# Chunked attention and a Gelu MLP on one core: k loaded in long runs, transposed by DMA and put in key order by GpSimd

## The chip, the cores and the metric

The kernel runs on one core of one Trainium2 chip. The metric is the device time of one launch in microseconds. The kernel's engines are TensorE (PE in the profile; PEld is its weight load), VectorE (DVE), ScalarE (ACT), GpSimd (POOL) and SyncE (SP), which issues nearly all DMAs; SPq is SP's queue of issues.

## The reference

q, k and v are float32 of shape 8 (batch) x 8 (heads) x 576 (positions) x 64. Attention runs inside chunks of 64 positions, so nine chunks per batch element and head:

```python
scores = (1.0 / np.sqrt(D)) * np.matmul(q_c, k_c.transpose(0, 1, 2, 4, 3))   # per chunk of 64
attn = softmax(scores)                                                        # over the 64 keys
out = np.matmul(attn, v_c)
x = out.transpose(0, 2, 1, 3).reshape(B * S, H * D)                           # 4608 x 512
h = x @ w_in                                                                  # 512 -> 2048
y = gelu_exact(h) @ w_out                                                     # 2048 -> 512
```

## The kernel before

**Tiles.** The 4608 token rows are cut into nine tiles of 512. Tiles 0 to 7 are the first eight chunks of one batch element; tile 8 gathers the ninth chunk of all eight batch elements. For each tile the attention gives x in bfloat16 (`x`, features on partitions); the first product (mm1, `mm1_slot`, L446) gives 16 slices of h, each followed by a Gelu on ScalarE (L448); the second product multiplies h by w_out.

**Order of the work.** The order is written out by hand under a manual schedule: each engine executes its instructions in the order in which the code emits them, and a helper puts the waits in. The main loop over t (L820) runs mm1 of tile t and then its second product in `phase`. The attention of the next tiles is put between the matmuls by two dictionaries: `e1` maps a slice number of mm1 to pieces of work that come ahead of it, `e2` does the same for the steps of the second product. `T0 = 2` is the last tile of a first regime. Tiles 1 and 2 take the attention of tile t+1 in their second product; tile 2 takes the scores of tile 4 at its end as well (step 12), so from tile 3 on the scores (`quad_S`) are two tiles ahead of mm1.

**Second product.** From tile 1 on `mm2_seven` computes the product of 2 x 2 blocks with seven block products instead of eight (steps s = 0 to 6, two sub-steps each, L564). Sums of blocks of h are made by DVE (`g_sum`, L487 and L500; they use s3_sb and the k_bd buffers as room), sums of blocks of w_out once by `weight_sum` (L475, into v_bd, during mm1 of tile 1). `keep` copies a bank of PSUM to an SBUF tile `kept` on ACT (L526), `done` adds a bank to a kept tile on DVE (L531) and stores it (L576). `last` copies the last bank to y_sb on ACT (L536) and stores it; for tile 2 it is put into the list `deferred` and executed ahead of slice 1 of tile 3. The SBUF tiles `kept` and `y_sb` share four buffers.

**The loads of q and k.** `load_qk` brings the float32 data of a tile into a staging buffer (`arrival`, six buffers for all kinds of loads). For q, the position (p j) goes to partition p with j = 4 neighbours in a row: runs of 4 x 64 floats, 1 KB, in one DMA of 1 MB (L114). For k from tile 2 on, `rows_128` (L124) puts the keys on partitions in blocks of 128: four DMAs of 256 KB in runs of 64 floats, 256 bytes; for tile 8 eight DMAs. GpSimd casts both to bfloat16, four instructions per tile and kind (`pool_cast_qk`; L164 for q, L162 for k). `flip` (L194) issues a DMA transpose from SP that puts head dimension on partitions, q_t and k_t with two buffers each. In q_t the positions of a chunk lie as (j, p); in k_t, because of the 128-key blocks, the 64 keys of a chunk lie side by side, and the scores take them as weights directly:

```python
st["kt"][rs, g * J + n, CH * c:CH * (c + 1)]     # L226: 64 keys of a chunk
```

v is loaded in 256-byte runs (`load_v_rows`, nine DMAs per tile) and cast by GpSimd (`cast_v_rows`, L200). Tiles 0 and 1 go another way (`att_Tq`, `att_Tk`: transposes on TensorE).

**Attention of a tile from 2 on.** `quad_S` (L225): 64 matmuls of 64 x 64 into four PSUM banks, exponentials on ACT (L232), partial row sums (`quad_part`, L248 and L251) and totals (`quad_total`) on DVE, or, for tiles 2 and 3, sums by a matmul (`quad_sums`); then `quad_av` (L310) and the product with the reciprocal sums into x (`quad_x`, L317; `quad_x_plain`, L303).

Of the kernel before, what the change touches and what calls it, by code (L numbers as in the profile page):

```python
# [11 lines left out]
def kernel(  # L12
# [10 lines left out]
    P = 128  # L23
# [54 lines left out]

    w_in_sb = consts.tile([P, KS, d_ff], bf16, name="w_in_sb")
    w_out_sb = consts.tile([P, FF, d_model], bf16, name="w_out_sb")  # L80
    w_in_v = moe_w_in.rearrange("(ks p) n -> p ks n", p=P)
    w_out_v = moe_w_out.rearrange("(f p) n -> p f n", p=P)

# [19 lines left out]
    def load_qk(t, nm, h0=0, h1=H):  # L103

        st = tiles[t]
        src = q if nm == "q" else k
        if nm + "f" not in st:
            st[nm + "f"] = stage_tile()[:].rearrange("p (h j d) -> p h j d", h=H, j=J)
            st[nm] = ld.tile([P, G, J, 2, D], bf16, tag=nm, name=f"{nm}_nat")
        raw = st[nm + "f"]  # L110
        if t > 1 and nm == "k":
            rows_128(t, src, raw, False)
        elif t < B:
            nc.sync.dma_start(raw[:, h0:h1], src[t, h0:h1, 0:MT, :].rearrange("h (p j) d -> p h j d", j=J))  # L114
        else:
            for b in range(B):
                nc.sync.dma_start(
                    raw[PC * b:PC * (b + 1), h0:h1],
                    src[b, h0:h1, MT:S, :].rearrange("h (p j) d -> p h j d", j=J))

    def rows_128(t, src, raw, swapped, parity=range(2)):

        def go(to, rows):
            nc.sync.dma_start(to, rows.rearrange("h key d -> key h d"))  # L124
        last = CT // 2 - 1
        if t < B and not swapped:
            for n in range(CT // 2):
                go(raw[:, :, n], src[t, :, P * n:P * (n + 1), :])
        elif t < B and 0 in parity:
            for n in range(CT // 2):  # L130
                go(raw[:, 0::2, n], src[t, 0::2, P * n:P * (n + 1), :])
        if t < B and swapped and 1 in parity:
            for n in range(last):
                go(raw[:, 1::2, n], src[t, 1::2, CH + P * n:CH + P * (n + 1), :])
            go(raw[0:CH, 1::2, last], src[t, 1::2, MT - CH:MT, :])
            go(raw[CH:P, 1::2, last], src[t, 1::2, 0:CH, :])
        if t == B:
            for b in range(B):
                for r in range(2 if swapped else 1):
                    c, n = place(r, b) if swapped else (b % 2, b // 2)  # L140
                    sel = slice(r, H, 2) if swapped else slice(0, H)
                    go(raw[CH * c:CH * (c + 1), sel, n], src[b, sel, MT:S, :])

    def place(r, i):

# [2 lines left out]
    def load_v_rows(t, parity=range(2)):  # L148
        if "vf" not in tiles[t]:
            tiles[t]["vf"] = stage_tile()[:].rearrange("p (h n d) -> p h n d", h=H, d=D)  # L150
        rows_128(t, v, tiles[t]["vf"], True, parity)

    def load_v(t):

# [3 lines left out]

    def cast_qk(t, nm, g, copy):
        st = tiles[t]  # L160
        if t > 1 and nm == "k":
            copy(st[nm][:, :, g], st[nm + "f"][:, :, g].rearrange("p (q r) d -> p q r d", r=2))  # L162
            return
        copy(st[nm][:, g].rearrange("p j r d -> p r j d"), st[nm + "f"][:, 2 * g:2 * g + 2])  # L164

    def cast_v(t, g, r, copies):
# [10 lines left out]

    def att_Tq(t, g, copy):
        tp = transposed(t, "q", g)
        qT = work.tile([P, CT, CH], bf16, tag="qT", name="qT", bufs=5)  # L180
        copy(qT[:].rearrange("p i (c j) -> p i c j", j=J), tp)
        tiles[t]["qT", g] = qT

    def att_Tk(t, g, copy):
# [5 lines left out]

    def flip(t, nm):
        st = tiles[t]
        st[nm + "t"] = flips.tile([P, G * J, P], bf16, tag=nm + "t", name=f"{nm}_t")
        nc.sync.dma_start_transpose(st[nm + "t"][:], st[nm][:].rearrange("p g j r d -> p (g j r d)"))  # L194

    def cast_v_rows(t, copy):
        st = tiles[t]
# [21 lines left out]
    def quad_S(t, banks, later=False, parts=True):  # L219

        st = tiles[t]
        s_ps = four_banks("s_ps", banks)
        for g2, u, g, n, r, c, o, rs, os in quadrants():
            i = 2 * n + c
            nc.tensor.matmul(s_ps[g2][c][os, u, :].rearrange("p (j c) -> p j c", j=J),  # L225
                             st["kt"][rs, g * J + n, CH * c:CH * (c + 1)],  # L226
                             st["qt"][rs, g * J:(g + 1) * J, i * PC:(i + 1) * PC],
                             start=True, stop=True, tile_position=(CH * r, CH * o))
        def exps(g2):
            for c in (1, 0):  # L230
                pT = work.tile([P, CT, CH], bf16, tag="pT", name="pT", bufs=5)
                nc.scalar.activation(pT[:].rearrange("p u (c j) -> p u c j", j=J),  # L232
                                     s_ps[g2][c][:].rearrange("p u (j c) -> p u c j", j=J), Act.Exp, scale=scale)
                st["pT", 2 * g2 + c] = pT
                if parts:
                    quad_part(t, g2, c)
        if later:
            return exps
        for g2 in range(2):
            exps(g2)  # L240
# [213 lines left out]
    HD = d_model // 2  # L454
    HM = MT // P // 2
    ADD, SUB = mybir.AluOpType.add, mybir.AluOpType.subtract
    s3_sb = consts.tile([P, HF, HD], bf16, name="s3_sb")

    def flat(tile, f):
        return tile[:].rearrange("p a b -> p (a b)").rearrange("p (f n) -> p f n", f=f)  # L460
# [38 lines left out]
        b = st["S", 2][part] if b is None else b[:, f]  # L499
        nc.vector.tensor_tensor(st["S", i][part], a, b, op=op)  # L500

    deferred = []

    def mm2_seven(t, hooks):

        st = tiles[t]
# [26 lines left out]

        def last():
            y_sb = ypool.tile([P, HM, HD], f32, tag="y", name="y_sb")
            nc.scalar.copy(y_sb[:], bank["a"][:])  # L536
            store_block(t, 1, 0, y_sb)

        first_done = lambda: done(0, 0, "b", "p1")
        if t <= T0:  # L540
# [5 lines left out]
                 ("d", summed(1), t_sum(1), lambda: keep("p5", "d")),  # L546
                 ("a", summed(3), t_sum(3), lambda: done(1, 1, "a", "p5")),
                 ("d", summed(4), w_block(1, 1), lambda: done(0, 1, "d", "u2")),
                 ("a", raw(1, 1), t_sum(4), (lambda: deferred.append(last)) if t == T0 else last)]
        for s, (name, left, right, then) in enumerate(steps):  # L550
            fresh = name not in bank
            for m in range(HM):
# [143 lines left out]
    with tc.manual_schedule():  # L696
# [114 lines left out]
        def flip_qk(t):  # L811
            for nm in "qk":
                flip(t, nm)

        def bring_qk(t):
            for nm in "qk":
# [3 lines left out]
        for t in range(1, NT):  # L820
# [3 lines left out]
            if t == 1:  # L824
                flip(2, "q")
                load_v_rows(2, (0,))
                flip(2, "k")
                for ms, y_sb in held:
                    store(0, ms, y_sb)
                held.clear()  # L830
                load_v_rows(2, (1,))
            elif t == T0:
                flip_qk(t + 1)
                load_qk(t + 2, "k")
                load_v_rows(t + 1)
                pool_cast_qk(t + 2)
            if n < NT:
                cast_v_rows(n, PO)
            if t == 1:
# [14 lines left out]
            if t <= T0:  # L854
                ov = [lambda m=m: quad_over(n, m) for m in range(G)]
                rx = [[lambda m=m: att_rc(n, m), lambda m=m: quad_x_plain(n, m)] for m in range(G)]
                e2 = {0: [exp, lambda: quad_S(n, ALONE, parts=False)] + g[1][:2], 2: g[1][2:],
                      4: [lambda: quad_sums(n)], 5: [ov[0]], 6: [ov[1]],
                      7: [ov[2], lambda: quad_av(n, ALONE)] + rx[0], 8: [ov[3]] + rx[1], 9: rx[2] + rx[3]}
                if t == 1:  # L860
                    for i, f in ((1, 6), (2, 7), (3, 8), (4, 9)):
                        e1[f] = [lambda i=i: weight_sum(i)] + e1.get(f, [])
                    e2[4].append(lambda: load_qk(4, "q"))
                    e2[11] = [gelu]
                else:
                    e2[12] = [lambda: quad_S(n + 1, ALONE), flip_next, gelu]
            else:
                e2 = {0: g[1][:2], 2: g[1][2:]}
                if n < NT:
                    if t == T0 + 1:  # L870
                        e1[1] = [lambda: deferred.pop()()]
                        e1[3] = [lambda: quad_total(n, DV)]
                    e1[5] = [lambda m=m: quad_rc(n, m // 2, m % 2) for m in range(1, G)]
                    later = []
                    e2 = {0: [exp, lambda: quad_av(n, EVEN if n + 1 < NT else ALONE), xs[0], g[1][0], xs[1], g[1][1]], 2: [flip_next],
                          4: [g[1][2]] + xs[2:],
                          13: [gelu]}
                    if n + 1 < NT:
                        e2[0].append(lambda: later.append(quad_S(n + 1, BESIDE, later=True)))
                        e2[0].append(lambda: later[0](0))  # L880
                        e2[2].append(lambda: later[0](1))
                        e2[10] = [lambda: quad_total(n + 1)]
# [33 lines left out]
```

## Time and profile before

| | |
|---|---|
| median of 3 runs | 279.09 us (278.34 to 282.12) |
| the profiled execution's own time | 278.27 us |
| span of the profiled execution | 276.4 us |
| TensorE busy, granted clock | 264.3 us, 96%; 1.00 |
| DVE, ACT, GpSimd busy | 166.6, 180.1, 92.5 us |
| DMA | 53.92 MB in 123407 packets, 97776 of them under 512 bytes |

The span runs from the first to the last instruction of the profiled execution. The page shows the busy time of each engine, then its busy share in 40 slices of 6.9 us, one digit per slice in tenths; PEclk is the granted TensorE clock. In a timeline a row is: start in us, length in us, engine, line, operation, output<-inputs, count; a bracket gives the idle time of the engine ahead of the row and what ended it. A busy TensorE is not TensorE at its peak, since the ends of matmuls are modelled.

### The profile page before, as it was taken

Reading aid. Unit: us, or ns where it says so; the run is one execution under the profiler, and the core shown is the slowest. Engines: PE = TensorE matmul, PEld = TensorE weight load, DVE = VectorE, ACT = ScalarE, POOL = GpSimd, SP = SyncE. Lnnn points to the kernel's source line nnn. Section 1 sums busy time; section 2 is a strip of 40 time slices with the busy share of each in tenths; the row PEclk is TensorE's granted clock in tenths of the full one; section 3 lists DMA queues with packets and bytes.
Section 4 is the critical chain, followed back from the end, with each engine's and each line's share of the span. In section 5 each row is a group of like instructions: output and inputs, shape, how many; then the busy total and the mean of one; then the engine's idle time right before and its main releaser. Section 6 shows DMA issues by size and latency. Waiting matters only on the chain.

```text
span 276.4 us, 6619 instructions
## 1 busy us (share of the span) xinstructions
PE 264.3 (96%) x2672; PEld 169.2 (61%) x2693; DVE 166.6 (60%) x279; ACT 180.1 (65%) x368; POOL 92.5 (33%) x146
## 2 busy tenths in 40 slices
PE   7699999999989999999989999999999999999994
PEld 2454455447844686458735874588458845874683
DVE  6866348875821679989705991598159915521522
ACT  3866758877846876774577567756776777346610
POOL 7869768832630515306303610451012000000000
PEclk9999999999999999999999999999999999999999
DMA  6999999998899899999999988979430310130014
GB/s 218 273 347 402 392 387 264 235 280 243 209 282 238 193 232 267 247 230 244 183 279 276 205 232 162 185 161 262 117 87 2 116 38 0 40 110 6 0 40 115
DMA packets 123407, 53.92 MB, mean 195 GB/s; under 512 B 97776, under 2 KB 120304, under 8 KB 123376
## 3 DMA queue, kind: packets, MB, share of 16 engines
q1 hardware_dynamic: 123072, 53.23, 75.6%
q8 instruction: 21, 0.34, 0.5%
q10 hardware_dynamic: 304, 0.26, 0.3%
q14 instruction: 10, 0.08, 0.1%
HBM read 36.70 MB, written 9.44 MB: 167 GB/s over the span
## 4 chain that ended last, share of the span: by engine, by line
PE 65%; SPq 15%; DMA 12%; issue 2%; ACT 2%; POOL 2%; DVE 1%; POOLq 0%; ACTq 0%
PE h_ps L446 30%; PE y_ps L564 25%; SPq L124 9%; PE y_ps L634 3%; DMA arrival<-in_q_dram 3%; PE h_ps L436 2%; SPq L157 2%; SPq L114 2%; DMA arrival<-in_moe_w_in_dram 2%; DMA arrival<-in_k_dram 2%; DMA k_t<-k_nat 2%; DMA arrival<-in_v_dram 2%; SPq L194 2%; DMA out_dram<-y_sb 2%; PE y_ps L598 1%
## 5 line engine op out<-in xcount | busy, mean ns | idle before, releaser
L446 PE MATMUL h_ps<-x,w_in_sb 128*128 128x512 bf16 x532 | 118.6, 379 | 1.9 <-ACT h L448 1.0
L448 ACT ACTIVATE h<-h_ps 128x512 bf16<-128x512 f32 x137 | 80.9, 598 | 31.5 <-PE h_ps L446 31.2
L446 PEld LDWEIGHTS <-w_in_sb 128*128 128x128 bf16 x548 | 53.6, 98 | 64.4 <-issue 1.3
L564 PEld LDWEIGHTS <-h 128*128 128x128 bf16 x384 | 36.9, 98 | 6.5 <-issue 1.7
L164 POOL CAST q_nat<-arrival 128x512 bf16<-128x512 f32 x31 | 18.7, 644 | 57.8 <-DMA arrival<-in_q_dram 40.9
L487 DVE TENSOR_TENSOR s_sb<-h 128x2048 bf16<-128x2048 bf16 x8 | 9.7, 1218 | 43.1 <-ACT h L448 43.1
L200 POOL CAST v_nat<-arrival 128x1024 bf16<-128x1024 f32 x14 | 16.8, 1203 | 39.9 <-DMA arrival<-in_v_dram 39.9
L564 PE MATMUL y_ps<-w_out_sb,h 128*128 128x256 bf16 x256 | 29.5, 273 | 0.3 <-issue 0.3
L564 PE MATMUL y_ps<-v_bd,k_bd 128*128 128x256 bf16 x256 | 29.6, 273 | 0.1
L526 ACT COPY kept<-y_ps 128x512 f32<-128x512 f32 (+1 forms) x26 | 14.4, 554 | 23.0 <-PE y_ps L564 22.6
L564 PEld LDWEIGHTS <-k_bd 128*128 128x128 bf16 x256 | 24.8, 98 | 3.4 <-issue 0.5
L162 POOL CAST k_nat<-arrival 128x512 bf16<-128x512 f32 x28 | 21.4, 787 | 9.5 <-DMA arrival<-in_k_dram 9.4
L531 DVE TENSOR_TENSOR kept<-y_ps,kept 128x512 f32<-128x512 f32 (+1 forms) x25 | 16.1, 651 | 12.9 <-PE y_ps L564 7.2
L694 ACT ACT_TABLE_LOAD x18 | 23.1, 1283 | 1.0 <-PEq L900 0.7
L500 DVE TENSOR_TENSOR k_bd<-h 128x1024 bf16<-128x1024 bf16 x16 | 11.5, 721 | 18.5 <-ACT h L448 18.5
L317 DVE TENSOR_TENSOR x<-av_ps,rc 128x512 bf16<-128x512 f32 x20 | 13.3, 685 | 5.2 <-PE av_ps L310 5.2
L232 ACT ACTIVATE pT<-s_ps 128x512 bf16<-128x512 f32 x28 | 14.8, 595 | 2.4 <-PE s_ps L225 2.4
L564 PE MATMUL y_ps<-v_bd,h 128*128 128x256 bf16 x128 | 15.3, 273 | 1.0 <-DVE kept L531 1.0
L564 PE MATMUL y_ps<-w_out_sb,s 128*128 128x256 bf16 x128 | 15.3, 273 | 0.0
L564 PE MATMUL y_ps<-v_bd,s_sb 128*128 128x256 bf16 x128 | 15.3, 273 | 0.0
L251 DVE TENSOR_REDUCE part<-pt 128x16 f32<-128x512 bf16 x20 | 13.7, 686 | 0.7
L564 PEld LDWEIGHTS <-s_sb 128*128 128x128 bf16 x128 | 12.5, 98 | 1.5
(103 smaller groups left out, 294.7 us busy)
## 6 DMA issues: line engine op xcount, KB each, us to landing
arrival<-in_v_dram SPq DMA_DIRECT2D x58, 128.0 KB, 3.1
arrival<-in_k_dram SPq DMA_DIRECT2D x28, 256.0 KB, 6.0
arrival<-in_q_dram SPq DMA_DIRECT2D x7, 1024.0 KB, 6.8
out_dram<-kept SPq DMA_DIRECT2D x21, 256.0 KB, 2.7
arrival<-in_moe_w_out_dram SPq DMA_DIRECT2D x4, 1024.0 KB, 11.6
arrival<-in_moe_w_in_dram SPq DMA_DIRECT2D x6, 512.0 KB, 7.5
out_dram<-y_sb SPq DMA_DIRECT2D x11, 256.0 KB, 2.7
arrival<-in_v_dram SPq DMA_DIRECT2D x28, 64.0 KB, 2.6
```

The source lines that it names most:

```text
L124: nc.sync.dma_start(to, rows.rearrange("h key d -> key h d"))
L162: copy(st[nm][:, :, g], st[nm + "f"][:, :, g].rearrange("p (q r) d -> p q r d", r=2))
L164: copy(st[nm][:, g].rearrange("p j r d -> p r j d"), st[nm + "f"][:, 2 * g:2 * g + 2])
L200: copy(st["v"][:, r::2], st["vf"][:, r::2])
L232: nc.scalar.activation(pT[:].rearrange("p u (c j) -> p u c j", j=J), s_ps[g2][c][:].rearrange("p u (j c) -> p u c j", j=J), Act.Exp, scale ...
L251: nc.vector.tensor_reduce(st["part", g2][:, c, :, :, 0], pt[:].rearrange("p n e u -> p n u e"), axis=mybir.AxisListType.X, op=mybir.AluOpT ...
L446: nc.tensor.matmul(h_ps[:], w_in_sb[:, ks, f * P:(f + 1) * P], tiles[t]["x"][:, ks, :], start=(ks == 0), stop=(ks == KS - 1))
L448: nc.scalar.activation(tiles[t]["h"][:, f, :], h_ps[:], Act.Gelu)
L526: nc.scalar.copy(kept[name][:, ms], ps[:])
L531: nc.vector.tensor_tensor(y_sb[:, ms], ps[:], y_sb[:, ms], op=ADD)
L564: nc.tensor.matmul(to, left(f, m), right[:, f], start=(fresh and (split or m == 0) and f == 0), stop=(f == HF - 1), skip_group_check=True)
L694: nc.scalar.activation(act_scratch[:], rest[:, 0:1], func)
```

## The change

- k of every tile is loaded as q is: one DMA of 1 MB in 1-KB runs (tile 8: eight DMAs), and cast with the instruction form of q.
- After the DMA transpose of k, four GpSimd copies per tile (`k_by_chunk`) write a new tile `k_c` (two buffers) in which the 64 keys of each chunk lie side by side in key order; they read k_t in steps of 128 bfloat16 elements. The scores read k_c. k_t has one buffer instead of two. The copies stand on GpSimd right behind the issue of the transpose in program order, for tile 2 ahead of the casts of v.
- The loads of q and k of tile 4 are both issued at step 4 of tile 1's second product (before: q there, k at the head of tile 2). The casts of tile 4 and the transposes of tile 3 stand at step 10 of tile 1's second product (before: at the head of tile 2). At the head of tile 2 come v's loads and casts of tile 3, then the transposes of tile 4.
- In tile 1 the last of four x products with its broadcast moves from step 9 to step 10.
- `last` of tile 2 is no longer deferred; it is done at once, by DVE. The partial row sums of tile 4 move from right behind its exponentials to ahead of slice 0 of tile 3.
- q transposed of tiles 0 and 1 is kept in s3_sb and not in buffers of its own.

```diff
+    s3_sb = consts.tile([P, FF // 2, d_model // 2], bf16, name="s3_sb")
...
-        if t > 1 and nm == "k":
-            rows_128(t, src, raw, False)
-        elif t < B:
+        if t < B:
             nc.sync.dma_start(raw[:, h0:h1], src[t, h0:h1, 0:MT, :].rearrange("h (p j) d -> p h j d", j=J))
...
-        if t > 1 and nm == "k":
-            copy(st[nm][:, :, g], st[nm + "f"][:, :, g].rearrange("p (q r) d -> p q r d", r=2))
-            return
         copy(st[nm][:, g].rearrange("p j r d -> p r j d"), st[nm + "f"][:, 2 * g:2 * g + 2])
...
-        qT = work.tile([P, CT, CH], bf16, tag="qT", name="qT", bufs=5)
+        qT = s3_sb[:, 2 * g:2 * g + 2].rearrange("p f (i c) -> p (f i) c", c=CH)
...
-        st[nm + "t"] = flips.tile([P, G * J, P], bf16, tag=nm + "t", name=f"{nm}_t")
+        st[nm + "t"] = flips.tile([P, G * J, P], bf16, tag=nm + "t", name=f"{nm}_t", bufs=2 if nm == "q" else 1)
...
+    def k_by_chunk(t, copy):
+        st = tiles[t]
+        st["kc"] = flips.tile([P, G, CT, CH], bf16, tag="kc", name="k_c")
+        for g in range(G):
+            copy(st["kc"][:, g].rearrange("p i (c j) -> p i c j", j=J),
+                 st["kt"][:, g * J:(g + 1) * J].rearrange("p j (i c) -> p i c j", i=CT))
...
-                             st["kt"][rs, g * J + n, CH * c:CH * (c + 1)],
+                             st["kc"][rs, g, i, :],
...
-            nc.scalar.copy(y_sb[:], bank["a"][:])
+            (DV if t == T0 else AC)(y_sb[:], bank["a"][:])
             store_block(t, 1, 0, y_sb)
...
-                 ("a", raw(1, 1), t_sum(4), (lambda: deferred.append(last)) if t == T0 else last)]
+                 ("a", raw(1, 1), t_sum(4), last)]
...
         def flip_qk(t):
             for nm in "qk":
                 flip(t, nm)
+            k_by_chunk(t, PO)
...
                 flip(2, "k")
+                k_by_chunk(2, PO)
...
             elif t == T0:
-                flip_qk(t + 1)
-                load_qk(t + 2, "k")
                 load_v_rows(t + 1)
-                pool_cast_qk(t + 2)
...
-                      7: [ov[2], lambda: quad_av(n, ALONE)] + rx[0], 8: [ov[3]] + rx[1], 9: rx[2] + rx[3]}
+                      7: [ov[2], lambda: quad_av(n, ALONE)] + rx[0], 8: [ov[3]] + rx[1], 9: rx[2], 10: rx[3]}
...
-                    e2[4].append(lambda: load_qk(4, "q"))
+                    e2[4].append(lambda: [load_qk(4, nm) for nm in "qk"])
+                    e2[10] += [lambda: pool_cast_qk(4), lambda: flip_qk(3)]
                     e2[11] = [gelu]
                 else:
-                    e2[12] = [lambda: quad_S(n + 1, ALONE), flip_next, gelu]
+                    e2[9] += e2.pop(10)
+                    e2[12] = [lambda: quad_S(n + 1, ALONE, parts=False), flip_next, gelu]
...
-                        e1[1] = [lambda: deferred.pop()()]
+                        e1[0] = [lambda m=m: quad_part(n, m // 2, m % 2) for m in (1, 0, 3, 2)]
                         e1[3] = [lambda: quad_total(n, DV)]
```

More of the change, by code (lines that the diff above doesn't have):

```diff
@@ L119, in load_qk, with rows_128 @@
                     src[b, h0:h1, MT:S, :].rearrange("h (p j) d -> p h j d", j=J))
-    def rows_128(t, src, raw, swapped, parity=range(2)):
+    def rows_128(t, raw, parity):
         def go(to, rows):
@@ L125, in rows_128 @@
         last = CT // 2 - 1
-        if t < B and not swapped:
+        if t < B and 0 in parity:
             for n in range(CT // 2):
[L128 to L132, printed above, removed]
+                go(raw[:, 0::2, n], v[t, 0::2, P * n:P * (n + 1), :])
+        if t < B and 1 in parity:
             for n in range(last):
-                go(raw[:, 1::2, n], src[t, 1::2, CH + P * n:CH + P * (n + 1), :])
-            go(raw[0:CH, 1::2, last], src[t, 1::2, MT - CH:MT, :])
-            go(raw[CH:P, 1::2, last], src[t, 1::2, 0:CH, :])
+                go(raw[:, 1::2, n], v[t, 1::2, CH + P * n:CH + P * (n + 1), :])
+            go(raw[0:CH, 1::2, last], v[t, 1::2, MT - CH:MT, :])
+            go(raw[CH:P, 1::2, last], v[t, 1::2, 0:CH, :])
         if t == B:
             for b in range(B):
[L139 to L142, printed above, removed]
+                for r in range(2):
+                    c, n = place(r, b)
+                    go(raw[CH * c:CH * (c + 1), r::2, n], v[b, r::2, MT:S, :])
     def place(r, i):
@@ L150, in load_v_rows @@
             tiles[t]["vf"] = stage_tile()[:].rearrange("p (h n d) -> p h n d", h=H, d=D)
-        rows_128(t, v, tiles[t]["vf"], True, parity)
+        rows_128(t, tiles[t]["vf"], parity)
     def load_v(t):
@@ L179, in att_Tq @@
         tp = transposed(t, "q", g)
-        qT = work.tile([P, CT, CH], bf16, tag="qT", name="qT", bufs=5)
-        copy(qT[:].rearrange("p i (c j) -> p i c j", j=J), tp)
+        qT = s3_sb[:, 2 * g:2 * g + 2].rearrange("p f (i c) -> p (f i) c", c=CH)
+        copy(qT.rearrange("p i (c j) -> p i c j", j=J), tp)
         tiles[t]["qT", g] = qT
@@ L456 @@
     ADD, SUB = mybir.AluOpType.add, mybir.AluOpType.subtract
-    s3_sb = consts.tile([P, HF, HD], bf16, name="s3_sb")
     def flat(tile, f):
@@ L500, in g_sum @@
         nc.vector.tensor_tensor(st["S", i][part], a, b, op=op)
-    deferred = []
     def mm2_seven(t, hooks):
```

## The prediction

> **What bounds the kernel now.** First the page: busy time, and TensorE (PE) with its granted clock over the slices.
>
> ```profile
> span 276.4 us, 6619 instructions
> PE 264.3 (96%) x2672; PEld 169.2 (61%) x2693; DVE 166.6 (60%) x279; ACT 180.1 (65%) x368; POOL 92.5 (33%) x146
> PE   7699999999989999999989999999999999999994
> PEclk9999999999999999999999999999999999999999
> ```
>
> PE is never below eight tenths after the start, at full clock. A change that leaves its matmuls alone can only fill or open holes between them. So the second view is the timeline of PE; the bracket is the idle time before a row.
>
> ```profile
> 63.61 0.71 PE L225 MATMUL s_ps<-q_t,k_t 64*64 64x64 bf16 x64
> 77.09 1.91 PE L564 MATMUL y_ps<-v_bd,h 128*128 128x256 bf16 x16 [0.87 <-DVE kept L531]
> 106.22 1.91 PE L564 MATMUL y_ps<-v_bd,h 128*128 128x256 bf16 x16 [0.16 <-DVE kept L531]
> 122.86 0.71 PE L225 MATMUL s_ps<-q_t,k_t 64*64 64x64 bf16 x64 [0.28 <-DMA k_t<-k_nat]
> 139.52 11.38 PE L446 MATMUL h_ps<-x,w_in_sb 128*128 128x512 bf16 x51 [1.03 <-ACT h L448]
> ```
>
> From 19 us on these are the holes, 2.34 us in all: the most that the middle of the kernel can give back, 0.8%. Row one has none: the scores of tile 2 start at 63.61 right behind a matmul. How early was their k? Third view, the timelines of SP, POOL and DVE ahead of 63.61.
>
> ```profile
> 43.51 0.44 SPq L114 DMA_DIRECT2D arrival<-in_q_dram  x1
> 44.06 6.91 SPq L124 DMA_DIRECT2D arrival<-in_k_dram  x4
> 56.07 1.83 SPq L194 DMA_TRANSPOSE k_t<-k_nat  x1
> ...
> 49.25 2.28 POOL L164 CAST q_nat<-arrival 128x512 bf16<-128x512 f32 x4 [0.87 <-DMA arrival<-in_q_dram]
> 51.48 1.23 POOL L162 CAST k_nat<-arrival 128x512 bf16<-128x512 f32 x2
> 52.88 3.16 POOL L162 CAST k_nat<-arrival 128x512 bf16<-128x512 f32 x2 [0.18 <-DMA arrival<-in_k_dram]
> ...
> 52.81 1.21 DVE L475 TENSOR_TENSOR v_bd<-w_out_sb 128x2048 bf16<-128x2048 bf16 x1
> 60.90 0.69 DVE L500 TENSOR_TENSOR k_bd<-h 128x1024 bf16<-128x1024 bf16 x1 [1.51 <-ACT h L448]
> ```
>
> Two casts of k take 0.61 us each; the two beside the weight sums L475 take 1.6 each: GpSimd and a DVE operation with two inputs in SBUF take turns. The transpose is issued at 56.07 and, by the tile view of k_t in this stretch, lands 4.0 later, at 60.1. That is 3.5 us ahead of its use: the slack this change spends.
>
> **The change part by part.** The profiled execution took 278.27 us, span 276.4; the median of the three runs is 279.09, 0.82 above it. I sum changes of the span and put them on the median.
>
> *Loads.* k of tiles 2 to 8 is one 1-MB DMA in 1-KB runs (eight for tile 8), not four in 256-byte runs. SP's issue falls from 6.91 us to about the 0.44 of q. Off PE's path: no PE hole names a load. Worth nothing by itself. The casts keep their number, 4 of 0.61 us per tile: nothing.
>
> *k in key order.* New: 4 GpSimd copies per tile, 128x512 bf16, read in steps of 256 bytes, between the landing of k's transpose and the scores, which now wait for the copies. No row shows such a read on GpSimd. The lower bound is the plain cast of as many elements, 0.61; the upper the longest cast of that shape, 1.61. A read by single elements resembles neither, so I take the middle, 1.11, and keep both. (The Trainium skill, GPSIMD Engine Reference, section 7, says that a GpSimd read with an inner step above 8 bytes costs about 2.9 cycles per element instead of 1.9; at the 1.2 GHz of that page 512 elements are an estimated 1.24 us, and four such copies would make the forecast below 280.3 instead of 279.8. No run so far shows it.) From tile 3 on, cover is there: k of tile 3 lands about 84, its copies follow the casts of tile 4 and end near 90, scores at 92.7; those of tile 5 land near 115, copies end near 119.5, the v casts behind them (2 of 1.04) near 121.6, just ahead of their use at 121.87. Without that cover each late us is a PE us.
>
> *Tile 2, where cover is thin.* (a) k lands whole behind q (49.2): 1.05 MB at the 312 GB/s of the stretch 47 to 50 is 3.4 us, 52.6; at the page's best slice, 402 GB/s, 51.8. Take 52.2, where the first two quarters were there at 51.48. (b) So one cast or two instead of two or more run free of L475 (52.81 on) and the others at 1.6: end between 51.9 + 1.2 + 3.2 = 56.3 and 52.3 + 0.6 + 4.8 = 57.7; take 57.0 (before: 56.04). (c) Transpose 4.0, lands 61.0. (d) Copies: three L500 sums at 60.9 to 63.0 take turns with them; casts beside L500 near 91 us took 1.11 and 1.01 instead of 0.61, so 0.45 more for three of the four: 4 x 1.11 + 1.35 = 5.8, end 66.9. (e) PE reaches the last sixteen score matmuls at 64.05: wait 2.85 us. PE works in order, so everything behind is as much later. Bounds: 56.3 + 4.0 + 4 x 0.61 = 62.7, no wait; 57.7 + 4.1 + 4 x 1.61 + 1.35 = 69.6, wait 5.5. Behind the copies on GpSimd stand v's casts of tile 2 (end near 69; used at 71.0 plus the wait): covered.
>
> *The hole at 77.09.* The last x product (0.69) and its broadcast (0.70) move from step 9 to step 10 of tile 1's second product, behind the sum that frees the bank. DVE reaches that sum at 75 instead of 76.36: -0.87. The x is then written by 77.0, its reader starts at 78: covered.
>
> *The hole at 122.86.* With loads of tiles 4 and 5 issued before the stores, SP is through with the loads of tile 5 and v of tile 4 by about 99 instead of 113; k's transpose of tile 5 waits for the third kept store and goes near 110, not 117.74, and the copies end before 122: -0.28. New there: k_t has one buffer, so SP stands at tile 4's transpose until tile 3's copies are done (near 90), with the loads of tile 5 behind it; they are due after 100.
>
> *The hole at 139.52.*
>
> ```profile
> 133.98 0.55 SPq L576 DMA_DIRECT2D out_dram<-y_sb  x1
> 138.39 0.58 ACT L536 COPY y_sb<-y_ps 128x512 f32<-128x512 f32 x1 [1.49 <-DMA out_dram<-y_sb]
> ```
>
> The deferred block of tile 2 was stored only at 133.98, and ACT waited for its buffer ahead of the Gelus. Now DVE evicts it at once (0.68) and SP stores it before the loads of tile 6. ACT is then free at 136.90; copy 0.58 and Gelu 0.60 end at 138.1, PE needs the bank at 138.5. Against it: DVE's four transposes with sums start behind the eviction (108.8 instead of 106.68), 2.1 us later; idle DVE time of 1.08 at 122.4 and 0.78 at 132.5 takes up most, 0.3 is left, which is the slack. -1.0, bounds 0 and -1.03. qT moves into a buffer that nobody uses until 58 us: nothing.
>
> Sum: -0.87 - 0.28 - 1.0 + 2.85 = +0.7. Median 279.8.
>
> **The rivals.** *In time*: the copies cost what a cast costs and k lands early, PE never waits: 279.09 - 2.15 = 276.9. For it: 3.5 us of slack, 2.43 of plain copies. Against: L475 and L500 stand on both ends. *Slow steps*: the 256-byte step costs several times a plain element. Decides from 2.35 us per copy, where the wait at the scores of tile 2 is 7.8 us (61.0 + 9.4 + 1.35 - 64.05) and the total 5.6 above before, 2%. At 3.0 us the copies end at 74.4, wait 10.3: 287.3. For it: no row of such a read; against: ACT's and DVE's copies of the same permutation (L188, L181: 578, 682 ns) are as quick as plain ones. *The clock falls in the wait*: PE does next to nothing between 63.6 and 66.9, and if it came back at half rate, the 32 matmuls behind it (3.67 us) would take as much again: 279.8 + 3.7 = 283.5. Against: the clock row shows no drop, though no hole there is longer than 1.1 us. (The Trainium skill, TensorE: Matmul & The Clock Gate, Part 1, has the clock halve after an idle window of about 3.4 us; by that rule the wait forecast here lies just below.) *Not sooner*: the transposes of tiles 4 and 5 still leave late, behind the stores that wait for DVE and the one k_t buffer; the holes of 0.28 and 1.03 stay: 281.1. Against: SP loses some 6 us of issue per tile.
>
> **How the numbers follow.** Forecast 0.56, in time 0.20, slow steps 0.12, clock 0.06, not sooner 0.06. The range 277.0 to 283.0 runs from "in time" to the upper bound of the wait (279.09 - 2.15 + 5.5 = 282.4) and leaves out some of "in time", most of "clock" and all of "slow steps". Two per cent, 5.6 us, is about what a measurement of this kernel tells from no change. Faster by that is shut out by 2.34 us of holes, 0.01; slower is "slow steps" with a part of "clock", 0.14; within 0.85.
>
> **What would show it.** Right: a hole of 2 to 4 us at the first scores L222 to L226 (tile 2), released by POOL k_c; copies of 0.9 to 1.3 us where DVE is idle; k's transpose of tile 2 issued near 57; no hole behind tile 1's last product, none at the scores of tile 5, none at the start of tile 4's first product. Wrong: copies of 0.6 us with no hole, copies above 2 us, a clock below 9 near 67 us, or a hole above 0.5 us at tile 3 or later.

## The result and the profile after

The changed kernel takes 293.91 us (median of 4 runs, 290.85 to 294.63), the kernel before 280.61 (4 runs). The ratio is 1.048 with a 95% interval of 1.035 to 1.062: slower by some 13 us, where 279.8 and "within 2%" were forecast. The profiled execution took 290.85 us, span 289.1 against 276.4. Runs of one kernel spread by 5 us and more, for a reason that stays open, so the ratios leave out those over 1.5% above the kernel's fastest, and three profiles below (tile 5's copies on ScalarE, the first with the whole path of k as before, k of tiles 2 and 5 as before) are of such longer runs, whose spans tell little.

The page first, the lines that answer to those shown of before. Two slices of the clock row now hold a 5, and TensorE has 6 us more of busy time (21 more of its matmuls are on record, the program has no more).

```profile
span 289.1 us, 6649 instructions
PE 270.3 (94%) x2693; PEld 172.1 (60%) x2693; DVE 175.9 (61%) x280; ACT 180.3 (62%) x367; POOL 124.3 (43%) x174
PE   6799999986999999975999999979999999999994
PEclk9999999995999999995999999999999999999999
```

The timeline of PE, the rows from 19 us on with more than 0.3 us of idle time ahead of them and the row behind each of the first two waits:

```profile
64.28 0.32 PE L225 MATMUL s_ps<-q_t,k_c 64*64 64x64 bf16 x16 [0.36 <-POOL k_c L193]
65.28 0.32 PE L225 MATMUL s_ps<-q_t,k_c 64*64 64x64 bf16 x16 [0.68 <-POOL k_c L193]
66.74 0.43 PE L225 MATMUL s_ps<-q_t,k_c 64*64 64x64 bf16 x16 [1.14 <-POOL k_c L193]
68.20 0.43 PE L225 MATMUL s_ps<-q_t,k_c 64*64 64x64 bf16 x16 [1.03 <-POOL k_c L193]
68.56 5.85 PE L561 MATMUL y_ps<-w_out_sb,h 128*128 128x256 bf16 x32
...
133.67 5.71 PE L561 MATMUL y_ps<-w_out_sb,h 128*128 128x256 bf16 x32 [5.16 <-DVE x L317]
...
195.13 1.05 PE L561 MATMUL y_ps<-w_out_sb,h 128*128 128x256 bf16 x8 [1.76 <-issue]
```

The two rows of 32 matmuls last 5.85 and 5.71 us where the same work took 3.67 before. The table of stretches says why: its columns are stretch, length, busy us of PE, PEld, DVE, ACT and POOL, granted clock, DMA share, GB/s.

```profile
64.00:68.50 4.50, 1.36 (x64) 1.00 (x64) 3.84 (x3) 3.01 (x5) 4.50 (x5) 0.75 0.72 166
68.50:72.00 3.50, 3.50 (x29) 2.47 (x18) 0.19 (x1) 1.09 (x2) 2.08 (x2) 0.50 0.80 262
133.60:137.00 3.40, 3.33 (x16) 2.37 (x16) 3.33 (x8) 0.00 (x0) 0.55 (x1) 0.50 0.79 167
```

After each long wait PE ran at half its clock. Laying equal rows of the two timelines side by side (start after minus start before) splits the 12.7 us of span. A stretch can gain more than the bracket of its hole, since the ends of rows are modelled:

| between | us | what |
|---|---|---|
| start to the scores of tile 2 | +0.2 | |
| scores of tile 2 | +4.1 | PE waits for the GpSimd copies |
| the 32 matmuls behind them | +2.2 | half clock |
| to the scores of tile 3 | -1.1 | the hole of 0.87 is gone |
| to the scores of tile 5 | -0.5 | the hole of 0.28 is gone |
| second product of tile 3 | +5.3 | PE waits for DVE's x of tile 4 |
| the 32 matmuls behind | +2.05 | half clock |
| to tile 4's attention | -1.2 | the hole of 1.03 is gone |
| near 190 us | +1.4 | a hole without a releaser, 0.33 before, 1.76 after |
| rest | +0.2 | |

So the three holes are gone, 2.8 us in all, and 15 us of waits and slow clock came with them. The first wait stands behind GpSimd, whose timeline shows the casts of tile 2's k and the copies behind them:

```profile
53.65 5.80 POOL L156 CAST k_nat<-arrival 128x512 bf16<-128x512 f32 x4 [0.40 <-PE h_ps L436]
63.17 4.97 POOL L193 COPY k_c<-k_t 128x512 bf16<-128x512 bf16 x4 [3.72 <-DMA k_t<-k_nat]
```

How did the second wait arise? The timelines of DVE and POOL ahead of 133.67, then one step of the chain of waits:

```profile
113.52 0.69 DVE L533 COPY y_sb<-y_ps 128x512 f32<-128x512 f32 x1 [1.40 <-PE y_ps L561]
118.52 5.64 DVE L262 COPY part<-part 32x32 f32<-32x32 f32 x8
132.94 0.68 DVE L317 TENSOR_TENSOR x<-av_ps,rc 128x512 bf16<-128x512 f32 x1
...
119.05 4.09 POOL L193 COPY k_c<-k_t 128x512 bf16<-128x512 bf16 x4 [9.87 <-DMA k_t<-k_nat]
...
119.08 1.08 DVE part L262
```

The timeline of DVE in the kernel before, for comparison:

```profile
111.08 1.50 DVE L262 COPY part<-part 32x32 f32<-32x32 f32 x8
122.38 0.69 DVE L317 TENSOR_TENSOR x<-av_ps,rc 128x512 bf16<-128x512 f32 x1 [1.08 <-PE av_ps L310]
```

Eight tiny copies of DVE, 1.50 us in all before, take 5.64. In the chain of waits three last 0.17 us each and the other five, from 119.08 on, about 1.0 each: the length of one GpSimd copy. DVE, which had already begun its sums 2.2 us later (behind the eviction at 113.52), reaches the x of tile 4 at 132.94. Only that product frees the PSUM bank into which PE's next matmul writes.

### The profile page after: what moved, and what is told of

It is laid out like the page before. It is cut to its first block, busy times and chain, and to the rows that moved or that the text cites. A ratio compares the mean times of both kernels' runs of the same rounds, so it can differ in the third digit from the quotient of the medians.

```text
span 289.1 us, 6649 instructions
## 1 busy us (share of the span) xinstructions
PE 270.3 (94%) x2693; PEld 172.1 (60%) x2693; DVE 175.9 (61%) x280; ACT 180.3 (62%) x367; POOL 124.3 (43%) x174
## 4 chain that ended last, share of the span: by engine, by line
PE 77%; DVE 9%; ACT 4%; POOL 4%; issue 3%; DMA 2%; SPq 0%; DVEq 0%; POOLq 0%
PE y_ps L561 33%; PE h_ps L446 33%; PE y_ps L631 3%; POOL k_nat L156 2%; DVE part L262 2%; PE h_ps L436 2%; DMA arrival<-in_k_dram 2%; ACT k_bd L180 2%; POOL k_c L193 1%; PE av_ps L310 1%; PE y_ps L595 1%; DVE part L251 1%; DVE rc L276 1%; PE s_ps L225 1%; PE av_ps L401 1%
## 5 line engine op out<-in xcount | busy, mean ns | idle before, releaser
L193 POOL COPY k_c<-k_t 128x512 bf16<-128x512 bf16 x28 | 31.2, 1157 | 39.2 <-DMA k_t<-k_nat 33.4
L561 PEld LDWEIGHTS <-h 128*128 128x128 bf16 x384 | 39.2, 103 | 14.1 <-issue 7.2
L561 PE MATMUL y_ps<-w_out_sb,h 128*128 128x256 bf16 x256 | 33.7, 296 | 6.9 <-DVE x L317 5.2
L486 DVE TENSOR_TENSOR s_sb<-h 128x2048 bf16<-128x2048 bf16 x8 | 10.7, 1337 | 41.3 <-ACT h L448 41.3
L156 POOL CAST q_nat<-arrival 128x512 bf16<-128x512 f32 x31 | 19.6, 671 | 31.7 <-DMA arrival<-in_q_dram 19.6
L156 POOL CAST k_nat<-arrival 128x512 bf16<-128x512 f32 x34 | 25.0, 770 | 8.1 <-DMA arrival<-in_k_dram 5.2
L499 DVE TENSOR_TENSOR k_bd<-h 128x1024 bf16<-128x1024 bf16 x16 | 12.4, 773 | 16.7 <-ACT h L448 16.7
```

Of the source, the lines that this page charges most:

```text
L193: copy(st["kc"][:, g].rearrange("p i (c j) -> p i c j", j=J), st["kt"][:, g * J:(g + 1) * J].rearrange("p j (i c) -> p i c j", i=CT))
L561: nc.tensor.matmul(to, left(f, m), right[:, f], start=(fresh and (split or m == 0) and f == 0), stop=(f == HF - 1), skip_group_check=True)
```

## Experiments

The first theory: each long wait comes from the GpSimd copies, at tile 2 because they stand ahead of the scores, at tile 5 because they hold DVE; behind each the clock halves. Rivals: one delay handed on, DVE's late start alone, or a clock that falls for another reason. Ratios below are to the kernel before on the same chip.

**k of tile 2 as before.**

```diff
+        if t == 2 and nm == "k":
+            for n in range(CT // 2):
+                nc.sync.dma_start(raw[:, :, n], src[t, :, P * n:P * (n + 1), :].rearrange("h key d -> key h d"))
...
-                             st["kc"][rs, g, i, :],
+                             st["kt"][rs, g * J + n, CH * c:CH * (c + 1)] if t == 2 else st["kc"][rs, g, i, :],
...
-                k_by_chunk(2, PO)
```

> The changed kernel with k of tile 2 alone as before: four loads in 256-byte runs, no GpSimd copies, scores on k_t. Theory (two separate waits, each with a fall of the clock behind it): the wait at the scores of tile 2 goes, 4.05 us, and with it the slow stretch behind it, 2.2 us; the wait of 5.2 us at 133 us and its slow stretch of 2.0 stay. Span 289.1 - 6.2 = 282.9. Rival (one delay handed on: tile 5's wait is the consequence of the late tile 2): both go, span about 276.

Measured: ratio 1.021 (1.013 to 1.029), span 284.6. The wait at tile 2 and its slow stretch are gone (32 matmuls in 3.67 us). The later wait is not, so it was not handed on. But it changed its place and its loser, as the timelines of PE and POOL show:

```profile
126.20 0.26 PE L316 MATMUL av_ps<-pT,v_nat 64*64 64x64 bf16 x1 [4.29 <-POOL v_nat L206]
127.19 1.07 PE L316 MATMUL av_ps<-pT,v_nat 64*64 64x64 bf16 x63 [0.73 <-POOL v_nat L206]
...
118.71 5.98 POOL L199 COPY k_c<-k_t 128x512 bf16<-128x512 bf16 x4 [9.46 <-DMA k_t<-k_nat]
```

Here DVE's small copies were done before GpSimd's began (1.51 us in all), and the GpSimd copies met DVE's block sums instead: 5.98 us for four, and the casts of tile 4's v behind them came 5 us too late for PE. The slow stretch followed again (5.03 us for 32 matmuls). Part of the theory fell: it is not always DVE's small copies that lose, but whichever of the two engines comes second.

**Tile 5's copies on ScalarE.**

```diff
+            if t != 5:
+                k_by_chunk(t, PO)
...
+                        for g4, f4 in enumerate((10, 11, 12, 14)):
+                            e1[f4] = e1.get(f4, []) + [lambda g4=g4: k_by_chunk(5, AC, (g4,))]
```

> The changed kernel with the four key-order copies of tile 5 alone on ScalarE, between the Gelus of tile 3's first product, instead of on GpSimd. Theory (GpSimd's copies hold DVE's small copies, five of eight taking 1.0 us instead of 0.17): the eight take 1.5 us instead of 5.6, x of tile 4 is 4.1 us earlier, the wait of 5.16 us falls to about 1 and the slow stretch behind it goes: span 289.1 - 4.1 - 2.0 = 283. Rival (the late start of DVE's sums behind the eviction is the cause, 2.2 us, and what GpSimd does is beside the point): the wait stays above 4 us and the span within 1 of 289.

Measured: ratio 1.015 (1.005 to 1.024). DVE's eight copies take 1.50 us, and no wait is left ahead of the second product:

```profile
119.51 1.50 DVE L263 COPY part<-part 32x32 f32<-32x32 f32 x8
131.04 3.67 PE L562 MATMUL y_ps<-w_out_sb,h 128*128 128x256 bf16 x32
```

The strided copies take 1.07 to 1.13 us on ScalarE too; they delay Gelus, which gives PE three holes of 0.9 us together. The span of 283 was missed: it is 287.4 in this execution, whose waits at tile 2's scores add up to 5.0 us and whose hole near 190 us is 3.2. The rival, DVE's late start alone, is out: it was left in, and the wait went.

**Eviction and partial sums of tile 4 as before.**

```diff
-            (DV if t == T0 else AC)(y_sb[:], bank["a"][:])
+            nc.scalar.copy(y_sb[:], bank["a"][:])
...
+                 ("a", raw(1, 1), t_sum(4), (lambda: deferred.append(last)) if t == T0 else last)]
...
+                    e2[12] = [lambda: quad_S(n + 1, ALONE), flip_next, gelu]
```

> The changed kernel with one part undone: tile 2's last block is deferred and evicted by ScalarE, and DVE's partial sums of tile 4 follow its exponentials, as before. Theory (the later start of 2.2 us is what puts DVE's eight small copies beside GpSimd's copies): they run ahead of the GpSimd copies and take 1.5 us in all; four later small copies may still meet them, up to 3.3 us; the wait of 5.16 us falls below 2 and the clock stays full, span 283 to 285. If lateness and lock simply add: the wait falls by 2.2 to 3.0 us, the slow stretch stays, span 287.

Measured: ratio 1.018 (1.008 to 1.028), span 282.1. The wait falls from 5.16 to 1.15 us and the clock stays full behind it:

```profile
129.33 3.65 PE L563 MATMUL y_ps<-w_out_sb,h 128*128 128x256 bf16 x32 [1.15 <-DVE x L317]
```

The eight small copies take 1.51 us; four later ones (L272) meet GpSimd and take 2.5, where they took 1.6 in the kernel before and 0.7 with tile 5's copies on ScalarE. So lateness and lock do not add. The 2.2 us are what puts DVE's small copies beside GpSimd's; either edit alone takes most of the wait away.

**PE kept busy in the wait of tile 2.**

```diff
-                e2 = {0: [exp, lambda: quad_S(n, ALONE, parts=False)] + g[1][:2], 2: g[1][2:],
+                e2 = {0: [exp] + ([lambda: keep_warm(14)] if t == 1 else []) + [lambda: quad_S(n, ALONE, parts=False)] + g[1][:2], 2: g[1][2:],
```

> The changed kernel with 14 extra matmuls of 512 columns (3.0 us at full clock) ahead of the scores of tile 2, whose result nobody reads; they fill the wait there and take no time from it. Theory (the fall of the clock is set off by the idle PE): the wait stays as long, to about 68.5, but the 32 matmuls behind it take 3.67 us instead of 5.85: 2.2 us less, span 287; the granted clock of the stretch behind is 1.00. Rival (the clock falls for another reason, such as power or what the other engines do): the matmuls take 5.85 all the same, span 289.

Measured: ratio 1.031 (1.021 to 1.042), span 286.9. From the timeline of PE, the filling (13 of its 14 matmuls are on record) and the row behind the scores:

```profile
64.50 3.19 PE L686 MATMUL warm<-rest 128*128 128x512 bf16 x13
69.20 3.67 PE L561 MATMUL y_ps<-w_out_sb,h 128*128 128x256 bf16 x32
```

The scores end at 69.3 us, not earlier than the 68.6 without the edit (the copies began 0.7 later here), and the 32 matmuls take 3.67 us at a clock of 1.00: the idle PE sets off the fall. At tile 5 this run had the wait for v (4.30 and 0.77 us), as with tile 2 undone.

**The whole path of k as before, the rest kept**, once with the new eviction and once with the old (`k_rows` makes the loads in 256-byte runs; the cast and two k_t buffers are as before too):

```diff
+        if t > 1 and nm == "k":
+            k_rows(t, src, raw)
...
-                             st["kc"][rs, g, i, :],
+                             st["kt"][rs, g * J + n, CH * c:CH * (c + 1)] if t > 1 else st["kc"][rs, g, i, :],
```

> The changed kernel with the whole path of k as before (256-byte runs, no copies, two k_t buffers), and every other part of the change kept: order of loads and transposes, tile 2's last block evicted by DVE at once, partial sums of tile 4 later, the moved x product. Theory (both waits come from the GpSimd copies): no wait at the scores of tile 2, none above 1 us near 128, clock full throughout; the holes of 0.87, 0.28 and 1.03 of the kernel before stay closed; span 274 to 275.5, 1 to 2 us below before. Rival (the reordered schedule costs time by itself, the 2.2 us by which DVE's sums are late): a wait of more than 2 us near 128, span above 277.

> As the run before, and tile 2's last block and the partial sums of tile 4 as before too: only the order of loads and transposes and the moved x product are left of the change. Theory: no wait near 128 at all, the hole of 0.87 closed, that of 1.03 closed if the store of the deferred block is now ahead of tile 6's loads; span 274 to 274.7, 0.6% under before and the fastest of all. Rival (the holes of 0.28 and 1.03 came from other work and return): span 275.5 to 276.

Measured: 0.996 (0.987 to 1.004) and 1.001 (0.996 to 1.007). No loss is left beyond the noise without the new path of k; the reordering by itself does not show a cost, but the gain forecast for it did not show either. Rows from the second kernel's PE timeline:

```profile
124.49 0.71 PE L241 MATMUL s_ps<-q_t,k_t 64*64 64x64 bf16 x64 [2.65 <-DMA k_t<-k_nat]
125.13 5.32 PE L579 MATMUL y_ps<-w_out_sb,h 128*128 128x256 bf16 x32
```

k's transpose of tile 5 came 2.65 us late in that run, by 1.90 in the first's, where the kernel before lost 0.28. "Clock full throughout" was missed too: behind both holes the 32 matmuls took 5.3 us instead of 3.67. Two holes of 1.38 and 1.26 us that the first had at tiles 3 and 4 left the clock full. That the short-run loads take the slack out of the new order, by keeping SP and the DMA engines busy, is a likely reason and was not tested.

**k of tiles 2 and 5 as before.** The same edit with `t in (2, 5)` for the condition.

> The changed kernel with k of tiles 2 and 5 alone as before; tiles 3, 4, 6, 7 and 8 keep the long runs and the GpSimd copies. Theory (the copies cost only where they stand ahead of a reader or beside DVE's late chain, tiles 2 and 5): both waits go, the clock stays full, span 275 to 277, with the hole without a releaser near 190 left. Rival (the copies cost wherever they run, through DVE): span above 279 with new holes at tiles 3 to 8.

Measured: 1.009 (0.998 to 1.020). The waits for the copies at tile 2 and for x at tile 5 are gone (at tile 2, 0.95 us of waiting for the transpose are left), but in this execution the theory that the copies cost only there fell:

```profile
64.80 0.71 PE L241 MATMUL s_ps<-q_t,k_t 64*64 64x64 bf16 x64 [0.95 <-DMA k_t<-k_nat]
93.94 0.32 PE L241 MATMUL s_ps<-q_t,k_c 64*64 64x64 bf16 x16 [0.83 <-POOL k_c L209]
95.41 0.32 PE L241 MATMUL s_ps<-q_t,k_c 64*64 64x64 bf16 x16 [1.14 <-POOL k_c L209]
96.86 0.43 PE L241 MATMUL s_ps<-q_t,k_c 64*64 64x64 bf16 x16 [1.14 <-POOL k_c L209]
```

PE comes to tile 3's scores at 93, not 98, and the copies of tile 3, from 91.2 on, are late by 3 us; the clock fell behind them (5.04 us for 32 matmuls). In the changed kernel the wait at tile 2 covers them. But the cover is thin and not the same in every execution: with tile 2 alone undone PE came there at 92.4, the copies had begun at 88.1, and the wait was 0.19 us. Whether every execution of this kernel has the wait is not on record.

**DVE's weight sums moved away from the casts of tile 2's k.**

```diff
-                    for i, f in ((1, 6), (2, 7), (3, 8), (4, 9)):
-                        e1[f] = [lambda i=i: weight_sum(i)] + e1.get(f, [])
+                    e2[0] = e2[0][:2] + [lambda: weight_sum(1), lambda: weight_sum(2)] + e2[0][2:]
+                    e2[2] = e2[2] + [lambda: weight_sum(3), lambda: weight_sum(4)]
```

> The changed kernel with DVE's four sums of blocks of w_out moved from tile 1's first product, where they stand beside the casts of tile 2's k, to behind the scores of tile 2. Theory (the casts take turns with them and so k's transpose leaves late): the four casts take 2.4 us instead of 5.8, the transpose of tile 2's k is issued near 56 instead of 59.5, the copies start near 59.8, the last scores of tile 2 end near 65 instead of 68.6, wait 0.5 to 1; the sums may cost up to 1 us later. Rival (the copies' own length is the cause): the wait stays above 2.5.

One run, 291.78 us. The timeline of POOL:

```profile
53.39 2.29 POOL L156 CAST k_nat<-arrival 128x512 bf16<-128x512 f32 x4 [1.07 <-DMA arrival<-in_k_dram]
61.14 6.30 POOL L193 COPY k_c<-k_t 128x512 bf16<-128x512 bf16 x4 [5.47 <-DMA k_t<-k_nat]
```

The casts fall from 5.80 to 2.29 us and the transpose is issued at 56.43, as expected. But the transpose took longer to land and the copies themselves stretch to 6.30, beside the block sums and then the moved sums; the waits at the scores still sum to 3.0 us. The rival's wait, above 2.5 us, came, but beside sums that the edit itself had moved there. Inconclusive between the two: both the late casts and the long copies count, and to take one away brought the other up.

**Copies that read side by side.**

```diff
-            copy(st["kc"][:, g].rearrange("p i (c j) -> p i c j", j=J),
-                 st["kt"][:, g * J:(g + 1) * J].rearrange("p j (i c) -> p i c j", i=CT))
+            copy(st["kc"][:, g].rearrange("p i c -> p (i c)"),
+                 st["kt"][:, g * J:(g + 1) * J].rearrange("p j e -> p (j e)"))
```

> The changed kernel with the GpSimd copies of k reading side by side instead of in steps of 256 bytes; their number, size and place stay, the keys come out in another order, so the scores are not the reference's. Theory (the step costs 0.45 us on each copy): a copy away from DVE takes 0.61 us, not 1.06; the scores of tile 2 end about 1.8 us earlier. Rival (a copy of bf16 costs 1.06 whatever its step): no change, 1.06.

One run, 282.7 us, span 280.9, clock 1.00 throughout.

```profile
118.44 2.29 POOL L193 COPY k_c<-k_t 128x512 bf16<-128x512 bf16 x4 [9.35 <-DMA k_t<-k_nat]
```

Four copies take 2.29 us away from DVE, against 4.09 with the step: 0.57 against 1.02 each. The scores of tile 2 end 2.2 us earlier; the waits there sum to 1.1 us, those at tile 5 to 2.0. In this one run, then, the step is worth some 8 of the 12.7 us of span, give or take the spread of the runs: 0.45 us per copy, carried by waits on two engines and the clock.

**k of tile 8 as before.** The edit above with `t in (8,)`.

> The changed kernel with k of tile 8 alone loaded as before (eight DMAs of 64 partitions in 256-byte runs) and no copies for it. Theory (the hole near 190 us without a releaser, 1.35 to 3.3 us in six kernels with the new tile 8 and at most 0.33 in those with the old, is PE waiting for its next instructions, whose fetch stands behind tile 8's loads): the hole falls below 0.5 us. Rival (it comes with the loads of v and the rest of the schedule): it stays between 1.3 and 3.3.

One run, 288.05 us. The row that stood at 195.13 after 1.76 us of idle time:

```profile
192.18 1.05 PE L577 MATMUL y_ps<-w_out_sb,h 128*128 128x256 bf16 x8 [0.41 <-issue]
```

The hole falls to 0.41, where eight kernels with the new tile 8, the changed one among them, show 1.35 to 3.3. Five kernels with the old tile 8 show 0.59 or less. It follows tile 8's loads (tile 8's copies run only after 200 us). That what PE waits for is a fetch of instructions is an inference, from a label that names no releaser; other DMA work was not varied.

**The moved x product alone, in the kernel before.**

```diff
-                      ... 8: [ov[3]] + rx[1], 9: rx[2] + rx[3]}
+                      ... 8: [ov[3]] + rx[1], 9: rx[2], 10: rx[3]}
```

> The kernel before with one part of the change: the last x product and its broadcast one step later in tiles 1 and 2. Theory: the hole of 0.87 us at 77 us closes, that of 0.16 too, nothing else moves: span about 275.4, 0.4% under before, which may not show against the spread of the runs.

Measured: 1.003 (0.998 to 1.008). The hole of 0.87 closes; in tile 2, where the scores of tile 4 come at step 12, they now wait 0.39 us for the moved product, and the spread hides the rest. "Nothing else moves" did not hold in this execution: tile 5's scores start at 122.79 (before: 122.86) after a hole of 0.99 instead of 0.28 us, for the transpose that they wait for came no earlier. What one hole gave was lost again in the next. No kernel tried beats the one before beyond its interval.

## Why the prediction was wrong

The sum forecast +0.7 us of span, and 12.7 came. Of the 12 between them, the second product of tile 3 has 5.3, the clock 4.25, the hole near 190 us 1.4, tile 2's wait 1.25 and the rest 0.4; the gains came out 0.65 larger than forecast.

*What bounds the kernel, and the ceiling on a gain*: right in kind. PE's holes were the only gain, though the list of them "from 19 us on" left out 0.17 us at 39.84 and 0.33 at 182.66, and the second of these grew. The three holes forecast to close did: 2.15 us forecast, 2.8 measured from start to start. For one only is the reason shown: the moved x product closes the hole of 0.87 by itself. The hole of 0.28 closed by luck: k's transpose of tile 5 went at 114.94, not "near 110", and its copies ended at 123.1, not "before 122", but PE came to these scores 4.9 us later than before. The hole of 1.03 stayed away also where the old eviction was put back, so the new eviction was not needed for it; PE was late in those kernels too, and what closes it stays open.

*Tile 2's wait*: the mechanism was right, the size 2.85 against 4.1 us. Terms (a) and (b) are the ones that were too small. (a) k was cast from 53.65, not 52.3, because q came later too: its casts, which stand ahead, ended at 53.25. (b) All four casts met the weight sums; they ended at 59.45, not 57.0, because "one cast or two" ran free in the sum and none did. (d) erred the other way: the copies took 4.97 us, not 5.8. They began behind the three sums that (d) has beside them and met the next three, from 64.59 on. The value taken for a copy, 1.11, was good: 1.02 to 1.06 measured away from DVE's two-input sums. The argument against slow copies was not: the quick copies of the same permutation (L188, L181) read PSUM, and ScalarE needed 1.07 to 1.13 us for it out of SBUF. The Trainium skill's rule (GPSIMD Engine Reference, section 7: about 2.9 cycles per element instead of 1.9) gave an estimated 1.24; it has the right sign, and the measured ratio, 1.02 to 0.57 us, is larger than the page's (some 1.5).

*The clock*: the rival that was right in kind, priced at 3.7 us and given 0.06. It cost 2.2 at tile 2 and 2.05 at tile 5. The step that failed is that it was left out of the sum: a clock row without a drop, in a kernel whose holes stay below 1.1 us, was set against a wait of 3 us, and "lies just below" an idle window was taken for safe. The Trainium skill (TensorE: Matmul & The Clock Gate, Part 1) speaks of an idle window of about 3.4 us. Less was enough here: the longest single hole at tile 2 was 1.14 us, with scores between the holes and PE busy for 1.36 of 4.5 us, and single holes of 1.90 and 2.65 us did the same in two other kernels. A wait cut in pieces is not safe.

*The hole at 139.52*: this is the step that failed worst. It did see DVE start "2.1 us later" and set idle time of DVE against it, down to 0.3. Two things are missing in it. It took the DVE rows from the trace of before, without the new GpSimd copies that the text itself puts at 115 to 119.5, beside them: 4.1 us. And it looked for the reader of that chain at 138.5 only; the first reader is the bank that x frees, where the second product of tile 3 starts, with 0.4 us of slack. Cost 5.3 us and 2.05 of slow clock.

*Cover from tile 3 on*: the place was named, "Without that cover each late us is a PE us", with v's casts 0.3 us ahead of their use. Taken as cover, it was the wait of two experiments, 5 us, and tile 3's in a third. Margins of tenths were booked as cover although (d) counted turns with DVE for tile 2 alone.

*Loads*: "Worth nothing by itself" missed 1.4 us near 190, at the hole that the list had left out.

## What to carry to other kernels

A new GpSimd pass is to be laid over DVE's timeline at every place where it will run, not only at the first: the two hold each other, and the one whose reader is nearest pays; count each tiny DVE operation that the pass meets at the length of a whole copy. A wait on PE can have a second price behind it: in these runs single holes of 1.90 us and more, and waits in pieces of 3 us and more, added 1.2 to 2.7 us of slow matmuls, and single holes up to 1.38 us added none. Idle matmuls put into the wait tell the two prices apart. A cover of a few tenths is a coin toss, and a wait that is taken away can uncover the next.

## What was not expected of the hardware

A DVE copy of 32x32 elements takes 0.17 us alone and 1.0 us when GpSimd copies run one after another: in these traces it ends with the copy under way each time. That agrees with the Trainium skill (SBUF — State Buffer, section "SBUF: two separate sides", on the port pair that VectorE and GpSimd share and hold for a whole instruction). The trace puts a price on it: the length of the other's instruction, not of one's own. In the other direction four GpSimd copies took 5.98 us beside DVE's two-input sums against 4.09. A strided copy in steps of 256 bytes is as slow on ScalarE (1.07 to 1.13 us) as on GpSimd (1.02 to 1.06); ScalarE's copies of the same permutation out of PSUM took 0.57 to 0.59 in the kernel before.
